# Half of the block sums and differences of a seven-product FFN made on GpSimd instead of VectorE, with every step's place in the issue list laid anew

## The chip, the cores and the metric

One core of a Trainium2 chip runs the whole program. The metric is the time of one execution on the device, in microseconds (us). A measurement of this kernel can tell about 0.5% from no change.

## What is computed

Local attention with a few global keys and a bias that falls with distance, followed by a two-layer FFN with a softplus between the layers. The reference, cut to what matters:

```python
# q, k, v: (4, 8, 768, 64) float32; n_global 8, n_local 96
scores = scale * q @ k.T
keep = (pos_k < n_global) | ((pos_q - pos_k >= 0) & (pos_q - pos_k < n_local))
scores = where(keep, scores + bias, -1e9)
a = softmax(scores)
x = (a @ v) laid out as (3072 tokens, 512)
h = x @ w_in                      # (512, 2048)
g = maximum(h, 0) + log1p(exp(-abs(h)))
out = g @ w_out                   # (2048, 512), float32
```

## The kernel before

The 3072 tokens are 24 blocks of 128 (six to a batch) and 12 chunks of two blocks. A block's attention needs the keys of its own block and the one before it; the eight global keys and values are copied over the first rows of the block before it (steps `gk` and `gv`, lines 271 and 275, small copies on GpSimd, ScalarE or VectorE). For each block and each half of the heads there are scores (`s`, `ss`, TensorE), the bias added (`ab`, `ac`, VectorE), an exponential (`e`, ScalarE), the product with V (`p`, TensorE) and a division by the row sum (`nm`, VectorE, into `xsf`). `xsf` is transposed into `XT` by TensorE or, from block 8 on, by a DMA from SyncE's queue (`y`).

The FFN takes a chunk of 256 tokens. Chunk 0, and the first layer of chunk 1, are made with plain products (`f`, `o`). From there on, both layers cut their matrices into 2 x 2 blocks and make the block product with seven products instead of eight, in the form that shares partial sums. That needs sums and differences of blocks:

- `x_dif` (step `ht`, line 512): four differences of blocks of `XT` to a chunk, 128x256, fp16, for the first layer; each of the four has a single buffer. `x_dif` 2 is made from 1, and 4 from 2.
- `w_sum` (step `hw`): the same of `w_in`, made once.
- `sum` (step `gs`, line 627): four sums and differences of blocks of G to a chunk, 128x1024, fp16, for the second layer; two buffers each. Sum 2 is made from 1, and 4 from 2. Sum 1 goes into output product 5, sum 2 into 6, sum 3 into 7 and sum 4 into 3.
- `w_dif` (step `wd`, line 612): four differences of blocks of `w_out`, in two halves of 128x1024, made once.

The first layer's seven products (step `h`, line 541, eight 128x128 matmuls each, twice per chunk) collect in PSUM; a copy (`hc`) and two additions (`hv`) join them, then exponential (`he`) and logarithm (`hl`) on ScalarE give G. The second layer's products (step `m`, line 657, eight matmuls of 256 columns) are copied (`ec`, ScalarE or VectorE) and added (`ev`, VectorE) into `osb`, which is stored (`st`).

Nothing is scheduled by a compiler. `ORDER` (line 707) is a list of step names, written out; each step appends its instructions to the queues of its engines, and every engine works its queue in that order, waiting by semaphore for what an instruction needs. So the list sets the order on all engines, and with it what stands behind a waiting instruction. A step's last number often chooses the engine. `BANKS` (line 187) tells which of three PSUM banks each temporary takes.

Loads of q, k, v and of the weights (`lq`, `lk`, `lv`, line 102, `wi`, `wo`) are issued from GpSimd's queue. To hold them back, a gate (step `g`, line 705) copies one element of G on GpSimd and so waits until that part of G is there.

Of the kernel before, what the change touches and what calls it, by code (L numbers as in the profile page):

```python
# [20 lines left out]
def kernel(  # L21
# [157 lines left out]
    def bias_part(half, part):  # L179
# [8 lines left out]
        "01201201210212012012012012102101200220201011021010112121010212210101211202210221"  # L188
        "011020201002110121120202112001221002"
# [313 lines left out]
    def x_dif(c, i):  # L503

        HD[c, i] = sums.tile([P, KH, P], F16, tag=f"x_dif{i}", name=f"x_dif{i}", bufs=1)
        a, b = {
            1: lambda: (x_block(c, 0, 1), x_block(c, 0, 0)),
            2: lambda: (x_block(c, 1, 1), HD[c, 1][:]),
            3: lambda: (x_block(c, 1, 1), x_block(c, 0, 1)),
            4: lambda: (x_block(c, 1, 0), HD[c, 2][:]),  # L510
        }[i]()
        nc.vector.tensor_tensor(HD[c, i][:], a, b, ALU.subtract)
# [105 lines left out]
    def g_sum(c, i):  # L618
# [8 lines left out]
        nc.vector.tensor_tensor(SM[c, i][:], a(), b(), op)  # L627
# [74 lines left out]
    def gate(s):  # L702
# [10 lines left out]
        fe1 nm3.0 wo0 nm3.1 s4.0 lv5 x3 wi6 f3 xc3.0 fe3 f9 ab4.0 s4.1 fe9 ab4.1 f0 wo1 t5 kc5.0
        e4.0 f8 qc5.0 gk5.1 s5.0 fe0 f2 ab5.0 f11 fe8 e4.1 gv4.0 wo2 fe2 e5.0 s5.1 fe11 f10 lp0
        p4.0 f13 hw1.0 fe10 hw2.0 f5 fe13 f4 lp1 nm4.0 p4.1 ab5.1 fe4 nm4.1 e5.1 fe5 hw3.0 f12
        gv5.2 x4 p5.0 lp4 nm5.0 o0 p5.1 lq6 nm5.1 xc4.0 lk6 hw1.1 wo3 fe12 o4 x5 f15 xc5.0 lp6
        wd1.0 f14 lp5 f7 ht2.1 fe14 fe15 lk7 h2.1.0 ht2.2 lq7 o1 hw4.0 wd1.1 fe7 hw3.1 hw2.1 lv6
        ht2.4 lq8 hc2.1.0.1 hw4.1 f6 h2.6.0 lp7 gs1.1 wd3.0 gs1.3 h2.2.0 fe6 lp2 o5 gs1.2 ht2.3
# [153 lines left out]
```

## Time and profile before

| | us |
|---|---|
| three runs | 203.16, 201.97, 202.85 |
| median | 202.85 |
| the profiled execution | 203.91 |
| its span, first to last instruction | 201.8 |

The granted clock of TensorE was 0.997 of full speed in that execution. The profile names the engines PE (TensorE matmuls), PEld (its weight loads, which run beside the matmuls), DVE (VectorE), ACT (ScalarE), POOL (GpSimd) and SP (SyncE). A row of a group gives line, engine, operation, output <- input, shape, count, then busy time and mean duration in ns, then the idle time before it. Durations overlap a little: an engine starts its next instruction before the last one's result has landed, so what an instruction costs an engine is the distance to the next start.

### The profile page before, as it was taken

What the parts mean: (1) busy time and instruction counts of PE and PEld (TensorE: products, weight loads), DVE (VectorE), ACT (ScalarE), POOL (GpSimd) and SP (SyncE); (2) the same over time, 40 slices, a digit from 0 to 9 for tenths busy, and PEclk for the clock granted to TensorE, in tenths of its full rate; (3) what the DMA queues carried; (4) which work ended last, traced back from release to release, by engine and by line L of the source; (5) the groups of instructions that cost most, each with busy time, mean ns of one, the idle gap of its engine ahead of it and who ended that gap; (6) DMA issues with size and microseconds to landing.
All of it is one profiled execution on the core that took longest, in us unless ns stands there. A gap on an engine that the chain in (4) does not pass through costs nothing.

```text
span 201.8 us, 6676 instructions
## 1 busy us (share of the span) xinstructions
PE 194.4 (96%) x2729; PEld 167.9 (83%) x2729; DVE 173.8 (86%) x403; ACT 173.5 (86%) x278; POOL 85.3 (42%) x142
## 2 busy tenths in 40 slices
PE   7989999999999999999999999989999999999993
PEld 2657887867989989989998998969999999999992
DVE  7557776999999999989999999979999998867571
ACT  2767699989999999999999999997999998898700
POOL 8997906860574648095264835451003110000000
PEclk9999999999999999999999999999999999999998
DMA  8999999999999999999999999999442512601123
GB/s 126 153 156 169 149 196 207 188 173 158 149 115 157 120 174 195 102 158 158 157 161 180 168 177 167 100 119 145 100 133 44 94 29 30 209 3 54 54 71 138
DMA packets 110622, 26.91 MB, mean 133 GB/s; under 512 B 101760, under 2 KB 108288, under 8 KB 110592
## 3 DMA queue, kind: packets, MB, share of 16 engines
q0 software_dynamic: 78080, 13.37, 98.3%
q1 hardware_dynamic: 31472, 12.85, 36.8%
q8 instruction: 21, 0.34, 0.7%
q10 hardware_dynamic: 1040, 0.26, 0.6%
q14 instruction: 9, 0.07, 0.2%
HBM read 27.26 MB, written 6.29 MB: 166 GB/s over the span
## 4 chain that ended last, share of the span: by engine, by line
PE 59%; DVE 20%; ACT 11%; DMA 5%; issue 3%; DVEq 0%; ACTq 0%
PE o L657 24%; PE hT L541 12%; PE p_ps L541 6%; PE hT L434 5%; PE x_ps L380 3%; DMA XT<-xsf 3%; ACT e_sb L571 3%; DVE sum L627 3%; ACT Pb L364 3%; PE s_ps L284 2%; DVE Z L353 2%; DMA k_f<-in_k_dram 2%; ACT G L575 2%; DVE w_dif L612 2%; DVE xsf L398 2%
## 5 line engine op out<-in xcount | busy, mean ns | idle before, releaser
L575 ACT ACTIVATE G<-e_sb 128x1024 f16<-128x1024 f32 x40 | 41.7, 1061 | 0.1
L541 PEld LDWEIGHTS <-w_sum 128*128 128x128 f16 x640 | 39.0, 98 | 3.2 <-issue 0.9
L364 ACT ACTIVATE Pb<-Z 128x1024 bf16<-128x1024 f32 (+1 forms) x40 | 39.9, 1002 | 0.0
L657 PEld LDWEIGHTS <-sum 128*128 128x128 f16 x352 | 32.7, 98 | 4.3 <-issue 0.6
L657 PE MATMUL o<-w_dif,sum 128*128 128x256 f16 x264 | 33.8, 273 | 0.6 <-DVE b L686 0.5
L541 PEld LDWEIGHTS <-w_in 128*128 128x128 f16 x480 | 29.4, 98 | 0.7 <-DMA XT<-xsf 0.2
L657 PEld LDWEIGHTS <-G 128*128 128x128 f16 x272 | 24.9, 98 | 3.1 <-issue 0.2
L571 ACT ACTIVATE e_sb<-hT 128x512 f32<-128x512 f32 x40 | 24.0, 602 | 2.9 <-PE hT L541 2.6
L541 PE MATMUL hT<-x_dif,w_sum 128*128 128x128 f16 x320 | 24.4, 219 | 0.3 <-DVE hT L551 0.3
L541 PE MATMUL hT<-XT,w_in 128*128 128x128 f16 x320 | 24.4, 219 | 0.0
L344 DVE TENSOR_TENSOR Z<-s_ps,biasA 128x1024 f32<-128x1024 f32 x19 | 23.1, 1216 | 1.1 <-PE s_ps L284 1.1
L275 POOL COPY v_t<-v_t 8x520 bf16<-8x520 bf16 x13 | 8.4, 645 | 33.7 <-PE x_ps L380 32.6
L657 PE MATMUL o<-w_out,G 128*128 128x256 f16 x168 | 21.8, 273 | 0.0
L102 POOL DMA_DIRECT2D v_t<-in_v_dram x24 | 21.5, 896 | 0.6 <-issue 0.5
L102 POOL DMA_DIRECT2D q_t<-in_q_dram x23 | 20.6, 895 | 2.2 <-DMA w_out<-in_moe_w_out_dram 1.4
L102 POOL DMA_DIRECT2D k_t<-in_k_dram x23 | 20.6, 900 | 1.6 <-issue 0.8
L398 DVE TENSOR_TENSOR xsf<-x_ps,rcp 128x256 f16<-128x256 f32 x44 | 18.7, 424 | 1.5
L380 PEld LDWEIGHTS <-Pb 128*128 128x128 bf16 x352 | 15.3, 98 | 2.5 <-issue 0.9
L380 PE MATMUL x_ps<-v_t,Pb 128*128 128x65 bf16 x324 | 17.1, 193 | 0.1
L434 PE MATMUL hT<-XT,w_in 128*128 128x256 f16 x128 | 15.6, 273 | 0.0
L566 DVE TENSOR_TENSOR e_sb<-hp,hT 128x512 f32<-128x512 f32 x20 | 13.6, 682 | 2.3 <-PE hT L541 2.3
L627 DVE TENSOR_TENSOR sum<-G 128x1024 f16<-128x1024 f16 x22 | 15.1, 687 | 0.0
(113 smaller groups left out, 381.4 us busy)
## 6 DMA issues: line engine op xcount, KB each, us to landing
out_dram<-osb SPq DMA_DIRECT2D x18, 256.0 KB, 4.1
v_t<-in_v_dram POOLq DMA_DIRECT2D x24, 128.0 KB, 5.9
k_t<-in_k_dram POOLq DMA_DIRECT2D x23, 128.0 KB, 5.9
q_t<-in_q_dram POOLq DMA_DIRECT2D x23, 128.0 KB, 5.8
w_out<-in_moe_w_out_dram POOLq DMA_DIRECT2D x4, 512.0 KB, 11.2
out_dram<-osb SPq DMA_DIRECT2D x10, 128.0 KB, 2.0
w_in<-in_moe_w_in_dram POOLq DMA_DIRECT2D x4, 256.0 KB, 7.1
w_in<-in_moe_w_in_dram POOLq DMA_DIRECT2D x2, 512.0 KB, 9.1
```

The costliest lines, as they stand in the source:

```text
L102: nc.gpsimd.dma_start(dst[n][:, :, 0:D], src[b, :, i * P : (i + 1) * P, :].rearrange("h s d -> s h d"))
L344: nc.vector.tensor_tensor(Z[:], buf[:, 0:8, :], biasA[:, half, :, :], ALU.add)
L364: nc.scalar.activation(Pb[:, 0:nreg, :], src, AF.Exp, scale=inv_sqrt)
L380: nc.tensor.matmul(x_b[:, lh, :], Pb[:, r, :], v_t[n - t][:, h, :], start=(t == 0), stop=(t == 1 or first),)
L398: nc.vector.tensor_tensor(xsf[:, h0 : h0 + 4, :], x_b[:, :, 0:D], rcp[:, h0 : h0 + 4][:, :, None].to_broadcast([P, 4, D]), ALU.mult,)
L434: nc.tensor.matmul(hT[:, j, :], w[:, m, fo : fo + P], XT[c][:, m, :], start=(j == 0 and m == 0), stop=(m == KM - 1), skip_group_check=(j > 0),
L541: nc.tensor.matmul(o[:, b, :], lhs(k, b), rhs[:, k, :], start=(i in (1, 5) and b == 0 and k == 0), stop=(k == KH - 1), skip_group_check=True,)
L566: nc.vector.tensor_tensor(t, HS[c, "p", u][:], HT[c, "x", u][:], ALU.add)
L571: nc.scalar.activation(o, t, AF.Exp)
L575: nc.scalar.activation(g_tile(c)[:, b0 : b0 + HB, :], HS.pop((c, i, u))[:], AF.Ln, bias=1.0)
L627: nc.vector.tensor_tensor(SM[c, i][:], a(), b(), op)
L657: nc.tensor.matmul(o, lhs[:, k, :], rhs(k)[:, c0:c1], start=(i in (1, 2, 5) and k == 0), stop=(k == NU - 1), skip_group_check=(i not in (1 ...
```

## The change

A new helper chooses between two engines, and `x_dif`, `w_dif_part` and `g_sum` get an argument for it. 18 of the 40 `x_dif`, 2 of the 8 `w_dif` halves and 22 of the 44 sums now have a 1 there. All other work is the same in kind and number; the list and the banks are written anew, and some steps' choice between VectorE, ScalarE and GpSimd changes with it (14 of the 40 `hc` copies are on VectorE instead of 7, and 10 of the small K and V copies instead of 2).

```diff
+    def sum_by(pool):
+        return nc.gpsimd.tensor_tensor if pool else nc.vector.tensor_tensor
...
-    def x_dif(c, i):
+    def x_dif(c, i, by=0):
...
-        nc.vector.tensor_tensor(HD[c, i][:], a, b, ALU.subtract)
+        sum_by(by)(HD[c, i][:], a, b, ALU.subtract)
...
-    def w_dif_part(i, part):
+    def w_dif_part(i, part, by=0):
...
-        nc.vector.tensor_tensor(t[i], a, b, ALU.subtract)
+        sum_by(by)(t[i], a, b, ALU.subtract)
...
-    def g_sum(c, i):
+    def g_sum(c, i, by=0):
...
-        nc.vector.tensor_tensor(SM[c, i][:], a(), b(), op)
+        sum_by(by)(SM[c, i][:], a(), b(), op)
...
-        p19.0 he8.11.0 ht8.4 hl7.1.1 m6.7 hv8.6.0 h8.7.0 nm19.0 hv8.7.0 ss20 ac20.0 p19.1 ab20.0
+        p19.0 h8.2.0 gs6.3.1 ht8.4.1 hc8.5.0.0 he8.11.0 m6.7 hl7.1.1 lq22 hv8.6.0 ec6.7.1 nm19.0
```

In the last line `gs6.3.1` is sum 3 of chunk 6 on GpSimd, and `m6.7` the product that takes it.

GpSimd's queue before, where the loads of block 23 are issued, around the sums of chunk 7 (`KT` and `v_t` copies are the small copies, `gate_t` the gates):

```order
L102 DMA k_t_89<-in_k_dram 128x8x64
L102 DMA q_t_83<-in_q_dram 128x8x64
L271 COPY KT<-KT 128x4x8
L275 COPY v_t_95<-v_t_94 8x520
L705 CAST gate_t<-G 1x1 x3
L275 COPY v_t_90<-v_t_94 8x520
L705 CAST gate_t<-G 1x1
L102 DMA v_t_92<-in_v_dram 128x8x64
```

The same place now; `sum_3209` and `sum_3238` are sums 1 and 2 of chunk 7, `sum_3358` is sum 4 of chunk 6, and the two `x_dif` are differences 3 and 1 of chunk 9:

```order
L102 DMA q_t_82<-in_q_dram 128x8x64
L102 DMA k_t_88<-in_k_dram 128x8x64
L708 CAST gate_t<-G 1x1 x3
L630 TENSOR_TENSOR sum_3209<-G 128x1024
L274 COPY KT<-KT 128x4x8
L278 COPY v_t_95<-v_t_94 8x520
L630 TENSOR_TENSOR sum_3238<-sum_3209,G 128x1024
L515 TENSOR_TENSOR x_dif_3281<-XT 128x256
L515 TENSOR_TENSOR x_dif_3305<-XT 128x256
L630 TENSOR_TENSOR sum_3358<-G,sum_2870 128x1024
```

Three sums and two differences now stand among the loads, gates and small copies, and what follows them on that queue follows their waits.

VectorE's queue before at sums 4 of chunk 6 and 1, 2, 3 of chunk 7 (`sum_3132`, `sum_3154`, `sum_3231`, `sum_3256`):

```order
L627 TENSOR_TENSOR sum_3132<-G,sum_2919 128x1024
L395 RECIPROCAL rcp<-x_ps 128x4
L398 TENSOR_TENSOR xsf<-x_ps,rcp 128x256
L627 TENSOR_TENSOR sum_3154<-G 128x1024
L566 TENSOR_TENSOR p_ps<-hp,hT 128x512
L353 TENSOR_TENSOR Z<-o,biasA 128x512
L627 TENSOR_TENSOR sum_3231<-sum_3154,G 128x1024
L627 TENSOR_TENSOR sum_3256<-G 128x1024
```

The same place now; of those four only sum 3 of chunk 7 (`sum_3234`) is left on VectorE:

```order
L356 TENSOR_TENSOR Z<-s_lo,biasA 128x512
L347 TENSOR_TENSOR Z<-s_ps,biasA 128x1024
L356 TENSOR_TENSOR Z<-o,biasA 128x512
L557 COPY hp<-p_ps 128x512
L569 TENSOR_TENSOR p_ps<-hp,hT 128x512
L630 TENSOR_TENSOR sum_3234<-G 128x1024
L569 TENSOR_TENSOR e_sb<-hp,hT 128x4x128
L356 TENSOR_TENSOR Z<-o,biasA 128x512
```

A copy of a product's block (`hp`) stands there that ScalarE made before, and three sums are gone from it; the one left has two inputs in SBUF, as `sum_3209` and `sum_3238` on GpSimd have, and stands between them in the list.

More of the change, by code (lines that the diff above doesn't have):

```diff
@@ L713 @@
[L713 to L718, printed above, removed]
@@ new lines @@
+        m1.2.1 h2.2.1 d8 nm6.0 p6.1 e7.1 hc2.5.1.1 ev1.2 nm6.1 e7.0 h2.6.1 g7 m1.6 hv2.6.1 p7.0
+        g15 he2.11.1 x6 gs1.4.0 lv8 he2.22.0 nm7.0 d9 hl2.1.0 h2.7.1 ec1.6.1 xc6.0 h2.3.1 p7.1
+        ss8 lq10 hv2.7.1 h2.4.1 m1.7 nm7.1 he2.12.1 ab8.0 he2.22.1 lk11 he2.21.1 lq11 ec1.7.0
+        gk9.2 gv8.2 x7 hl2.0.1 h3.1.0 xc7.0 ac8.1 m1.4 lv9 ac8.0 ss9 d10 ec1.4.0 e8.0 p8.0 ac9.0
+        st0.1 lq15 e8.1 ht3.1.1 ac9.1 nm8.0 h3.5.0 ht3.2.1 hc3.1.0.1 m1.5.0 hc3.5.0.1 h3.6.0
+        hl2.1.1 h3.2.0 d11 he3.11.0 ev1.5 hv3.6.0 m1.3 ab9.0 lq13 h3.3.0 ht3.3.1 h3.1.1 ev1.3
@@ new lines @@
+        gk10.0 p8.1 gv9.0 e9.1 lq12 h3.7.0 he3.12.0 hc3.1.1.1 e9.0 ht3.4.1 nm8.1 m2.1.0 h3.2.1
+        he3.11.1 hv3.7.0 gs2.1.1 h3.4.0 lk12 p9.0 lv10 h3.6.1 gs2.3.0 g21 nm9.0 h3.5.1 he3.21.0
+        gs2.2.0 p9.1 ec2.1.1 ss10 he3.22.0 m2.6 nm9.1 hc3.5.1.1 y8 hv3.6.1 hl3.0.0 st0.0 h3.3.1
+        ab10.0 ec2.6.1 h3.7.1 ac10.1 m2.7 he3.12.1 lv11 e10.0 y9 gv10.2 ec2.7.1 hl3.0.1 ac10.0
+        gk11.2 ss11 gs2.4.1 lk13 lv12 hv3.7.1 ac11.0 ac11.1 h4.1.0 d12 e10.1 m2.4 h3.4.1 p10.0
+        ec2.4.1 he3.22.1 m2.2.1 hc4.1.0.1 ab11.0 nm10.0 he3.21.1 m2.5.0 lq14 ht4.1.0 ev2.2
@@ new lines @@
+        h4.2.0 e11.0 g27 lk15 g23 p10.1 he4.11.0 g13 gv11.0 h4.5.0 d13 ht4.2.1 ev2.5 nm10.1
+        h4.6.0 hc4.5.0.1 ht4.3.1 m2.3 gv18 hv4.6.0 p11.0 lq17 h4.7.0 ev2.3 nm11.0 e11.1 h4.3.0
+        hv4.7.0 ss12 ht4.4.1 p11.1 h4.4.0 hl3.1.1 hl3.1.0 ac12.0 nm11.1 gs3.1.0 he4.12.0 h4.1.1
+        m3.1.0 he4.21.0 ab12.0 hc4.1.1.1 h4.5.1 gs3.2.0 h4.6.1 h4.2.1 he4.22.0 hc4.5.1.1 y10
+        e12.0 gs3.3.1 ec3.1.0 m3.6 ac12.1 lk14 he4.11.1 lv13 lk16 g11 st1.1 y11 e12.1 p12.0
+        st1.0 hv4.6.1 ss13 h4.7.1 nm12.0 h4.3.1 ac13.0 ec3.6.1 gk14.0 hl4.0.0 m3.7 gs3.4.1
@@ new lines @@
+        hv4.7.1 p12.1 h4.4.1 ht5.1.1 g17 hl4.1.0 h5.1.0 lq16 he4.12.1 ac13.1 ec3.7.0 he4.22.1
+        m3.4 st2.0 ht5.3.0 ht5.2.0 he4.21.1 hc5.1.0.1 d14 ab13.0 ht5.4.0 lv14 hl4.1.1 h5.5.0
+        lq18 hc5.5.0.0 m3.5.1 ev3.5 h5.6.0 hl4.0.1 hv5.6.0 nm12.1 e13.0 h5.2.0 gs4.1.0 d15
+        he5.11.0 m3.3 lk17 h5.7.0 h5.3.0 ev3.3 p13.0 y12 ss14 hv5.7.0 nm13.0 e13.1 h5.4.0
+        he5.12.0 h5.1.1 g19 ec3.4.1 ac14.1 he5.22.0 gs4.2.1 m3.2.0 lq19 ac14.0 ab14.0 h5.5.1
+        p13.1 he5.21.0 ev3.2 hc5.1.1.1 e14.1 lk18 hc5.5.1.0 h5.2.1 h5.6.1 he5.11.1 hv5.6.1
@@ new lines @@
+        gv14.0 m4.1.0 e14.0 nm13.1 d16 ec4.1.1 hl5.1.0 gk15.2 ss15 gs4.4.0 h5.7.1 m4.6 hv5.7.1
+        hl5.0.0 ec4.6.1 h5.3.1 st2.1 he5.12.1 ac15.0 gs4.3.1 ac15.1 p14.0 h5.4.1 h6.1.0 nm14.0
+        m4.2.1 ab15.0 y13 gk16.0 ht6.1.0 hc6.1.0.1 e15.1 m4.7 p14.1 lv17 h6.2.0 ht6.2.0 g37
+        ec4.7.0 ht6.3.0 he5.21.1 h6.5.0 he5.22.1 lv15 lq20 h6.6.0 lq21 he6.11.0 m4.4 ev4.2
+        ht6.4.1 hc6.5.0.1 d17 ss16 nm14.1 hl5.0.1 hv6.6.0 y14 gk17.0 h6.7.0 ec4.4.1 g43 ac16.0
+        h6.3.0 lv16 m4.5.0 e15.0 hv6.7.0 hl5.1.1 h6.4.0 gv13 g31 ac16.1 h6.1.1 gv15.0 gs5.3.1
@@ new lines @@
+        ev4.5 m4.3 ab16.0 he6.12.0 ev4.3 lk20 d18 p15.0 he6.21.0 hc6.1.1.1 ss17 e16.0 st3.0
+        nm15.0 gs5.1.0 h6.2.1 e16.1 gs5.2.0 p15.1 nm15.1 m5.1.0 st3.1 y15 he6.11.1 h6.6.1
+        ec5.1.1 h6.5.1 m5.6 ac17.0 gv16.1 p16.0 ac17.1 hc6.5.1.1 st4.0 h7.1.0 gk13 hv6.6.1
+        he6.22.0 ec5.6.1 h6.3.1 h6.7.1 g29 e17.1 lv18 g39 nm16.0 p16.1 ab17.0 he6.12.1 m5.7
+        hv6.7.1 m5.5.1 hc7.1.0.0 lk19 g25 hl6.0.0 lk21 ec5.7.1 gs5.4.1 nm16.1 gv17.2 d19 ev5.5
+        ht7.1.0 h6.4.1 e17.0 h7.2.0 ht7.2.1 he6.22.1 lv19 p17.0 he6.21.1 m5.3 y16 h7.5.0 h7.6.0
@@ new lines @@
+        nm17.0 he7.11.0 ev5.3 hl6.1.0 g33 ss18 m5.4 ht7.3.1 hl6.0.1 hc7.5.0.0 ht7.4.1 d21 g51
+        gk18 hv7.6.0 ac18.1 p17.1 ac18.0 g35 ab18.0 hl6.1.1 e18.1 h7.7.0 h7.3.0 he7.12.0 g47
+        hv7.7.0 gs6.1.1 nm17.1 ss19 g45 h7.4.0 h7.1.1 ac19.0 ec5.4.1 ac19.1 he7.21.0 gs6.2.0
+        m6.1.0 hc7.1.1.1 h7.5.1 h7.2.1 lk23 gk20.2 e18.0 hc7.5.1.0 h7.6.1 lv20 y17 m5.2.1
+        hl7.0.0 p18.0 e19.1 hv7.6.1 ab19.0 h7.7.1 hv7.7.1 lq23 ec6.1.1 h7.3.1 ev5.2 lv21 m6.6
+        nm18.0 h7.4.1 he7.22.0 d20 he7.11.1 ht8.3.1 h8.1.0 ht8.1.0 he7.12.1 p18.1 e19.0 he7.21.1
@@ new lines @@
+        ac21.0 ht9.1.1 he8.22.0 ec7.6.1 he8.21.1 h9.1.0 m6.5.1 hc9.1.0.1 nm20.0 h9.5.0 ab21.0
+        ev6.5 p20.1 hc9.5.0.0 gk22.1 gs6.4.1 h9.2.0 e21.0 e21.1 ht9.2.0 nm20.1 he8.22.1 gv21.2
+        st5.1 he9.11.0 m6.3 ev6.3 g49 h9.6.0 hl8.1.0 m7.7 lv23 hl8.0.1 p21.0 lv22 ht9.4.0 ss22
+        hv9.6.0 ec7.7.0 h9.3.0 d23 nm21.0 m7.4 he9.12.0 h9.7.0 ab22.0 g65 p21.1 ac22.0 hv9.7.0
+        gk23.2 ec7.4.1 m7.2.0 hl8.1.1 h9.4.0 e22.0 gs7.4.1 ac22.1 gs8.1.1 nm21.1 gv22.2 ev7.2
+        ss23 ac23.0 gs8.2.1 he9.21.0 ac23.1 y21 h9.5.1 hc9.5.1.1 y20 h9.1.1 hc9.1.1.1 m7.5.0
@@ new lines @@
+        h9.6.1 ev7.5 g59 m8.1.1 st6.1 hv9.6.1 e22.1 p22.0 hl9.0.0 h9.2.1 ec8.1.1 h9.7.1 st7.1
+        he9.22.0 nm22.0 h9.3.1 m8.6 hl9.1.0 p22.1 he9.12.1 hv9.7.1 h9.4.1 ab23.0 he9.11.1
+        he9.21.1 e23.0 g63 ht10.1.0 ht10.2.0 gv12 nm22.1 ec8.6.1 h10.1.0 gs8.3.1 m7.3 e23.1
+        hc10.1.0.0 gv23.2 h10.5.0 h10.6.0 hc10.5.0.0 m8.7 hv10.6.0 ev7.3 ht10.3.0 he9.22.1 g61
+        ec8.7.1 p23.0 h10.2.0 st6.0 nm23.0 g73 hl9.0.1 h10.3.0 h10.7.0 ht10.4.1 he10.12.0
+        hv10.7.0 p23.1 m8.2.0 he10.11.0 h10.4.0 nm23.1 ev8.2 h10.1.1 hl9.1.1 h10.5.1 m8.5.0
@@ new lines @@
+        gs8.4.0 g69 he10.21.0 gk12 y22 hc10.5.1.1 gs9.1.0 y23 gs9.2.1 hc10.1.1.1 m8.4 hl10.0.0
+        ev8.5 ec8.4.1 h10.6.1 hv10.6.1 ht11.1.0 h10.2.1 m9.1.1 ec9.1.0 g67 he10.11.1 h10.7.1
+        h10.3.1 m8.3 ht11.2.0 h11.1.0 hv10.7.1 gs9.4.1 he10.22.0 he10.12.1 h10.4.1 ev8.3
+        he10.21.1 m9.6 hc11.1.0.0 h11.6.0 ec9.6.1 st8.1 hl10.0.1 h11.5.0 gs9.3.0 he10.22.1
+        h11.2.0 m9.7 ht11.4.0 m10.1.0 hc11.5.0.0 hv11.6.0 ht11.3.0 h11.7.0 ec9.7.0 hl10.1.0
+        hl10.1.1 hv11.7.0 m9.4 gs10.1.0 ec9.4.0 h11.3.0 ec10.1.0 he11.11.0 gs10.2.0 h11.4.0
@@ new lines @@
+        he11.12.0 he11.21.0 h11.1.1 m9.5.1 hc11.1.1.1 h11.5.1 ev9.5 hl11.0.0 hc11.5.1.0
+        he11.22.0 h11.6.1 st8.0 m10.6 hv11.6.1 st7.0 h11.2.1 ec10.6.0 h11.7.1 he11.11.1 gs10.3.0
+        hv11.7.1 h11.3.1 m9.3 ev9.3 h11.4.1 he11.12.1 gs10.4.0 he11.22.1 m10.7 m9.2.1 ec10.7.0
+        m10.4 ev9.2 hl11.1.0 he11.21.1 m10.5.1 hl11.0.1 hl11.1.1 gs11.1.0 ev10.5 ec10.4.1
+        m11.2.2.1 m11.1.0 m10.3 gs11.2.0 ev10.3 gs11.3.1 st9.1 st9.0 ec11.1.1 m11.6 gs11.4.1
+        m10.2.1 ec11.6.1 ev10.2 gk19 m11.7 ec11.7.0 m11.5.1 m11.4 ev11.2.1 ev11.5 st10.0
@@ L794 @@
+        st11.0.1 m11.2.2.0 m11.3 st10.1 ev11.2.0 ec11.4.1 st11.1 ev11.3 st11.0.0
     """
```

103 lines of the change are left out of this document (22 added, 81 removed).

## The prediction

> **What bounds the kernel now.** I read the page's head first, then busy time by stretch.
>
> ```profile
> span 201.8 us, 6676 instructions
> PE 194.4 (96%) x2729; PEld 167.9 (83%) x2729; DVE 173.8 (86%) x403; ACT 173.5 (86%) x278; POOL 85.3 (42%) x142
> ```
> ```profile
> core 0: us, PE busy (x) PEld busy (x) DVE busy (x) ACT busy (x) POOL busy (x), PEclk, DMA share, GB/s
> 50.00:158.00 108.00, 106.40 (x1678) 96.77 (x1673) 103.74 (x227) 104.58 (x170) 50.14 (x90) 1.00 1.67 142
> 158.00:202.00 44.00, 40.44 (x521) 37.61 (x518) 31.42 (x68) 30.21 (x48) 1.37 (x5) 0.99 0.23 73
> ```
>
> From 50 to 158 us (output product 1 of chunk 1 to that of chunk 8) TensorE, VectorE and ScalarE are all busy 96 to 99%, and GpSimd 46%. After 158 VectorE is busy 71% and TensorE has the say, so less VectorE work there is worth little. A busy TensorE is not a full one; the chain of waits gives what a step takes when nothing holds it (start us, us, what):
>
> ```profile
> 65.61 0.87 PE o L657 x8
> 66.48 0.89 PE hT L541 x16
> 68.57 0.24 PE x_ps L380 x8
> ...
> 155.37 0.33 PE s_ps L284 x8
> ...
> 155.93 0.98 PE o L657 x8
> ...
> 158.04 0.87 PE o L657 x8
> ```
>
> The list has, between those two products, in both kernels alike, 100 first-layer products (0.89/2 = 0.445 us each), 48 output products (0.87), 32 P.V steps (0.24, five at a batch's start half), 16 score steps (155.93 - 155.37 = 0.56, two of them half) and two transposes (0.2): 44.5 + 41.8 + 7.1 + 8.4 + 0.4 = 102.2 us. So TensorE loses 5.8 us of 108 there. That is the most that relief of VectorE and ScalarE in this stretch can bring. Where GpSimd waits, by the list of waits (us in total, times, longest):
>
> ```profile
> POOL v_t L275 <- PE x_ps L380: 32.6, 8, 9.0
> POOL KT L271 <- PE o L284: 24.5, 7, 5.3
> POOL gate_t L705 <- ACT G L575: 16.4, 5, 5.0
> ```
>
> Its idle time is 73 us of waiting, in order, for copies and gates whose data is not there yet; it is free time only if something can be put ahead of those waits.
>
> **The change, part by part.** *What VectorE loses and gains.* Groups by shape (busy, mean ns), and a run without waits from the timeline:
>
> ```profile
> L627 DVE TENSOR_TENSOR sum<-G 128x1024 f16<-128x1024 f16 x22 | 15.1, 687 | 0.0
> L512 DVE TENSOR_TENSOR x_dif<-XT,x_dif 128x256 f16<-128x256 f16 x20 | 5.7, 284 | 0.1
> L554 ACT COPY hp<-p_ps 128x512 f32<-128x512 f32 x15 | 8.8, 590 | 0.4 <-PE p_ps L541 0.2
> L554 DVE COPY hp<-p_ps 128x512 f32<-128x512 f32 x5 | 3.4, 684 | 0.3 <-PE p_ps L541 0.3
> ```
> ```profile
> 42.12 0.68 DVE L627 TENSOR_TENSOR sum<-G 128x1024 f16<-128x1024 f16 x1
> 42.72 0.68 DVE L627 TENSOR_TENSOR sum<-sum,G 128x1024 f16<-128x1024 f16 x1
> 43.32 0.28 DVE L512 TENSOR_TENSOR x_dif<-XT 128x256 f16<-128x256 f16 x1
> 43.53 0.68 DVE L566 TENSOR_TENSOR p_ps<-hp,hT 128x512 f32<-128x512 f32 x1
> ```
>
> From start to start a sum costs VectorE 0.60 us and an x_dif 0.21. By the orders, 22 of 44 sums, 18 of 40 x_dif and 2 of 8 w_dif halves go to GpSimd. Between the two products the count on VectorE falls from 25 sums, 28 x_dif and 1 w_dif to 11, 12 and 0: 14 x 0.60 + 16 x 0.21 + 0.60 = 12.4 us. The new list also moves work the other way: 5 more copies of a 128x512 block (0.60 each) leave ScalarE for VectorE, and 7 more of the small K and V copies leave GpSimd and ScalarE for it (about 0.2 each, as the x_dif, the shortest row here): 4.4 us back. Net relief of VectorE 8.0 us of 103.7; ScalarE loses 5 x 0.59 = 2.9 of 104.6.
>
> *What a sum costs on GpSimd.* No row shows a two-input operation there. The nearest are its copies (min/median/max ns):
>
> ```profile
> L275 POOL COPY v_t<-v_t x13: 607/611/1069, 14.1 to 159.6; 8x520 bf16<-8x520 bf16 x13
> ```
> ```profile
> L271 POOL COPY KT<-KT x12: 201/211/437, 14.9 to 138.0; 128x32 bf16<-128x32 bf16 x12
> ```
> ```profile
> L705 POOL CAST gate_t<-G x32: 177/179/499, 50.3 to 165.3; 1x1 bf16<-1x1 f16 x32
> ```
> ```profile
> L102 POOL DMA_DIRECT2D v_t<-in_v_dram x24: 876/885/958, 3.2 to 154.2; - x24
> ...
> DMA to landing us min/median/max: 3.5/5.9/10.6
> ```
>
> (611 - 211)/(520 - 32) = 0.82 ns per element and 0.185 us fixed. One pass over 1024 elements gives 1.02 us, two passes (one per input) 1.86, three (the result too) 2.70; for an x_dif 0.39, 0.60 or 0.81. I take 1.86 and 0.60, since two tensors must be read, and keep the others as ends. The Trainium skill, "GPSIMD Engine Reference", section 3.1, gives 4497 ns for an add of 2048 fp32; half of it, an estimate of 2.25 us, would bring the sum below to about 209 us.
>
> *Fill of GpSimd.* In the stretch it gets 16 sums, 2 w_dif and 16 x_dif: 18 x 1.86 + 16 x 0.60 = 43.1 us, beside 43 loads x 0.89, 27 gates x 0.19, 7 K copies x 0.21 and 6 V copies x 0.61 = 48.6. Together 91.7 us of 108, or 85%; by the high price 61.6 + 48.6 = 110.2, more than the stretch. Each sum waits in the queue for G, for its partner and for a free buffer, and loads, gates and copies stand behind it. A load lands 5.9 us after its issue and is listed well ahead of its use, so I cost late loads at nothing; with the high price that cover is gone.
>
> *The meeting of the two engines.* Two places of the timeline, VectorE and GpSimd:
>
> ```profile
> 104.98 0.67 DVE L627 TENSOR_TENSOR sum<-G,sum 128x1024 f16<-128x1024 f16 x1
> ...
> 112.35 0.82 DVE L627 TENSOR_TENSOR sum<-G 128x1024 f16<-128x1024 f16 x1
> 113.09 0.68 DVE L353 TENSOR_TENSOR Z<-s_lo,biasA 128x512 f32<-128x512 f32 x1
> ```
> ```profile
> 105.06 1.07 POOL L275 COPY v_t<-v_t 8x520 bf16<-8x520 bf16 x1
> ...
> 112.02 0.61 POOL L275 COPY v_t<-v_t 8x520 bf16<-8x520 bf16 x1 [3.82 <-PE x_ps L380]
> ```
>
> The copy that began 0.08 us into a sum took 1.07 instead of 0.61, that is, it stood until the sum was nearly done. The sum that began 0.28 us before the end of a copy took 0.82 instead of 0.68. The maxima of the K copy (437 ns) and the gate (499) point the same way: whichever comes second waits for the first. The Trainium skill, "SBUF — State Buffer", section "Who interferes with whom", makes it a rule: with two inputs in SBUF, VectorE's instruction and a GpSimd one that reads SBUF exclude each other, and the second blocks until the first finishes. The trace agrees for the copy; the sum was held 0.14 us, less than the 0.28 that the whole of the copy would give.
>
> Now the holder would be three times longer. GpSimd's 43.1 us are 40% of the stretch, and 23 two-input operations (11 + 12) stay on VectorE. One that arrives at random during a GpSimd one waits on average (18 x 1.86^2 + 16 x 0.60^2)/(2 x 43.1) = 0.79 us: 23 x 0.40 x 0.79 = 7.3 us. By the low price it is 23 x 0.23 x 0.43 = 2.3 us, by the high one 23 x 0.57 x 1.15 = 15 us. The middle value takes back 7.3 of the 8.0 us of relief, and as waits at places where the list has none.
>
> *Later sums.* A sum that took 0.68 us from start to end takes 1.86. In the list eight of the GpSimd sums stand at most 2.4 us of TensorE work ahead of their product: none ahead of product 7 of chunk 6, one 0.45 us product ahead of product 3 of that chunk, 1.1 to 2.4 us for the others. If each started where it stands, the shortfalls would be 1.86 + 1.41 + 0.74 + 0.3 + 0.1 + 0.1 = 4.5 us. But a place in the list is not yet a start. In the kernel before, sum 2 of chunk 10 stands directly ahead of product 6, and yet nothing waited (VectorE's timeline, then the chain of waits):
>
> ```profile
> 182.07 0.69 DVE L627 TENSOR_TENSOR sum<-sum,G 128x1024 f16<-128x1024 f16 x1
> ```
> ```profile
> 182.21 1.75 PE o L657 x16
> ```
>
> Product 6 is the second half of those 16 matmuls: it began 1.0 us after the sum, since TensorE was one product behind. Counting 0.9 us for that leaves 0.96 + 0.51 = 1.5. I take the middle, 3 us, and it falls on TensorE, the engine that sets the end.
>
> *Other stretches.* Up to 50 us, two w_dif halves, a sum and an x_dif leave VectorE, and loads and first products come in another order; the page gives no sign for it, and I take 0. After 158 us VectorE is idle 29% of the time, so its relief there brings nothing; the two sums of chunk 11 on GpSimd are needed only after other products: 0.
>
> **Sum.** The profiled execution took 203.9 us, its span 201.8 and 2.1 around it; the three timed runs have a median of 202.85. VectorE 0 (8.0 - 7.3, and what is left is not enough to move TensorE), ScalarE 0, late sums +3.0: 206.9 against 203.9, or 205.9 against the median. I put 206.
>
> **Rivals.** *A, the forecast:* the exclusion eats the relief and late sums add 1.5 to 5.5 us: 204 to 208.5. For it speaks the 1.07 us copy; against it, that its meetings are counted as random, and the order may keep them apart.
>
> *B, faster:* the sums cost GpSimd about one pass and rarely meet VectorE's. Then VectorE gains 8.0 - 2.3 = 5.7 us and ScalarE 2.9, and TensorE gets back more than half of its 5.8 us, 3.4: 199.5 (197 to 201.8). It decides once the waits of VectorE's 23 operations stay under some 3 us in total. For it speak VectorE's and ScalarE's 96% and 97% and GpSimd's 46%; against it, the two slowed rows.
>
> *C, no change:* relief and waits cancel, and the sums come early enough: 202 to 203.8.
>
> *D, GpSimd becomes the bound:* at 2.70 us a sum it has 110.2 us of work in a stretch of 108, and not all of its waiting for TensorE (57 us in all now) can vanish. With 5 to 10 us of it left the stretch takes 115 to 120, and the whole 210 to 215. For it speak the 85% at the middle price and the copies' 0.82 ns; against it, that a third pass for the result is likely to run beside the reads.
>
> **Chances.** A 0.45, B 0.30, C 0.13, D 0.12. A measurement here tells about 0.5% from no change, 201.8 to 203.9. All of B lies below: faster 0.30. C and the low edge of A (0.04) are the same: 0.17. The rest, 0.41 + 0.12, is slower: 0.53. A alone goes from 204 to 208.5; for 8 in 10 the range runs from 199, leaving out the lower part of B (0.10), to 212.5, leaving out the upper half of D (0.06).
>
> **What would show it.** Right: a GpSimd sum near 1.9 us; VectorE sums and x_dif with means well over 687 and 284 ns, some over 1.5 us; VectorE busy still about 96% from 50 us to product 1 of chunk 8, with fewer instructions; TensorE waiting for sum on GpSimd, at product 7 of chunk 6 first. B is right if those means stay and VectorE falls under 92%; D, if GpSimd is busy over 95% and its loads land late. The forecast is wrong if the sums take 1 us, or if waits of TensorE for GpSimd do not show.

## The result, and the profile after

The changed kernel takes 209.9 us (median; 208.95 to 210.23), the kernel before 202.9 us beside it: 1.035 times as long, with a 95% interval of 1.030 to 1.039. So it is 7.0 us slower; the forecast was 206.0, +3.1 against the median. The granted clock was 1.00 in the profiled execution (208.95) and 0.992 in the other three; up to 1 us of the 7.0 may be that. The page of the changed kernel, and its busy time by stretch (product 1 of chunk 8 now begins at 161.1):

```profile
span 207.1 us, 6708 instructions
PE 193.6 (93%) x2727; PEld 166.9 (81%) x2729; DVE 172.7 (83%) x374; ACT 171.1 (83%) x272; POOL 145.6 (70%) x177
```
```profile
50.00:161.00 111.00, 106.88 (x1686) 97.38 (x1687) 105.33 (x217) 102.91 (x164) 91.92 (x115) 1.00 1.39 135
161.00:207.00 46.00, 41.38 (x534) 38.19 (x531) 31.25 (x62) 29.66 (x48) 14.40 (x14) 1.00 0.24 79
```

VectorE has 29 instructions fewer and is busy for almost the same time, 172.7 us instead of 173.8: what is left on it has become longer. GpSimd's 91.9 us of work in the middle are near the 91.7 that the prediction had summed, in part by luck: durations overlap a little here too, and with the overlap counted twice the moved operations alone took 47.2 us, where 43.1 were summed. The groups by shape say which operations are longer (mean ns behind the comma):

```profile
L630 DVE TENSOR_TENSOR sum<-sum,G 128x1024 f16<-128x1024 f16 x7 | 7.8, 1112 | 0.0
L515 DVE TENSOR_TENSOR x_dif<-XT 128x256 f16<-128x256 f16 x12 | 6.9, 577 | 0.1
L278 DVE COPY v_t<-v_t 8x520 bf16<-8x520 bf16 x4 | 3.4, 848 | 0.4 <-PE x_ps L383 0.4
L569 DVE TENSOR_TENSOR e_sb<-hp,hT 128x512 f32<-128x512 f32 x20 | 13.6, 680 | 1.6 <-PE hT L544 1.5
...
L630 POOL TENSOR_TENSOR sum<-G 128x1024 f16<-128x1024 f16 x11 | 23.4, 2127 | 19.5 <-ACT G L578 17.5 <-ACT G L456 2.0
L515 POOL TENSOR_TENSOR x_dif<-XT,x_dif 128x256 f16<-128x256 f16 x10 | 7.0, 702 | 5.5 <-DVE x_dif L515 2.9 <-PE x_ps L383 1.7 <-issue 0.6
```

A sum on GpSimd takes 2.13 us. Sums, differences and small copies on VectorE have means well over those of the same operation alone; the additions with an input in PSUM (`e_sb`) have not. Taking each VectorE operation against what its kind takes undisturbed in this trace (the median for sums and differences, the shortest for the few copies), sixteen are held, for 12.4 us: sums 4.3, differences 3.6, V copies 2.3, K copies 1.7, `w_dif` 0.5. What TensorE waited for, and then GpSimd (us in total, times, longest):

```profile
PE s_ps L287 <- DVE Z L345: 3.1, 1, 3.1
PE o L660 <- DVE osb L699: 2.1, 2, 1.3
PE hT L544 <- DVE e_sb L569: 1.0, 2, 0.6
PE hT L544 <- DVE hT L554: 0.6, 2, 0.3
```
```profile
POOL sum L630 <- ACT G L578: 17.5, 4, 16.2
POOL sum L630 <- DVE sum L630: 10.1, 3, 6.2
```

Not one wait of TensorE is for a sum on GpSimd. After the first 10 us its waits come to 7.8 us, in the kernel before to 2.2; the spans of the two traces differ by 5.3. Six of the waits, 6.4 us together, are for VectorE and stand behind an operation that was held; the other new ones are of 0.3 us or less, for ScalarE and for a load. The largest, on VectorE, GpSimd and TensorE:

```profile
45.94 3.69 DVE L630 TENSOR_TENSOR sum<-sum,G 128x1024 f16<-128x1024 f16 x1
...
46.02 0.90 POOL L102 DMA_DIRECT2D k_t<-in_k_dram  x1
46.92 2.15 POOL L615 TENSOR_TENSOR w_dif<-w_out,w_out 128x1024 f16<-128x1024 f16 x1
...
51.59 0.40 PE L287 MATMUL s_ps<-QT,KT 64*128 64x128 bf16 x8 [3.12 <-DVE Z L345]
```

The sum on VectorE ends 0.56 us after GpSimd's `w_dif` half, and the score step's bias addition stands behind it, with two of VectorE's own `w_dif` halves between. The second largest is behind one of the small copies:

```profile
112.38 1.88 DVE L278 COPY v_t<-v_t 8x520 bf16<-8x520 bf16 x1
...
111.99 2.12 POOL L630 TENSOR_TENSOR sum<-G 128x1024 f16<-128x1024 f16 x1
...
114.64 1.03 PE L660 MATMUL o<-w_out,sum 128*128 128x256 f16 x8 [1.33 <-DVE osb L699]
```

Where TensorE stands, by the start of its products in the two traces (us, before and after): product 1 of chunk 1 at 50.1 and 52.6, of chunk 8 at 157.9 and 161.1, product 3 of chunk 11 at 197.4 and 202.7. So 2.5 us were lost before the stretch that the prediction reasoned about, 0.7 in it, and 2.1 after it. (The trace of before is of an execution 1 us over the median, that of the changed kernel of one 1 us under it.)

### The profile page after: what moved, and what is told of

It is laid out like the page before. It is cut to its first block, busy times and chain, and to the rows that moved or that the text cites. A ratio compares the mean times of both kernels' runs of the same rounds, so it can differ in the third digit from the quotient of the medians.

```text
span 207.1 us, 6708 instructions
## 1 busy us (share of the span) xinstructions
PE 193.6 (93%) x2727; PEld 166.9 (81%) x2729; DVE 172.7 (83%) x374; ACT 171.1 (83%) x272; POOL 145.6 (70%) x177
## 4 chain that ended last, share of the span: by engine, by line
PE 63%; DVE 18%; ACT 7%; DMA 6%; issue 4%; POOL 1%; DVEq 0%; ACTq 0%
PE o L660 24%; PE hT L544 17%; PE p_ps L544 6%; PE x_ps L383 4%; DMA w_in<-in_moe_w_in_dram 4%; PE s_ps L287 3%; PE hT L437 3%; DVE sum L630 2%; DMA k_f<-in_k_dram 2%; DVE x_dif L515 2%; ACT Pb L367 2%; DVE e_sb L569 2%; DVE Z L347 2%; DVE w_dif L615 2%; DVE v_t L278 1%
## 5 line engine op out<-in xcount | busy, mean ns | idle before, releaser
L630 POOL TENSOR_TENSOR sum<-G 128x1024 f16<-128x1024 f16 x11 | 23.4, 2127 | 19.5 <-ACT G L578 17.5
L544 PEld LDWEIGHTS <-w_in 128*128 128x128 f16 x480 | 28.7, 98 | 3.2 <-DVE e_sb L569 1.1
L287 PEld LDWEIGHTS <-KT 64*128 64x128 bf16 x352 | 10.0, 94 | 8.6 <-issue 5.9
L630 POOL TENSOR_TENSOR sum<-G,sum 128x1024 f16<-128x1024 f16 x7 | 14.9, 2126 | 1.7 <-DVE sum L630 1.6
```

What stands on the lines that cost most here:

```text
L287: nc.tensor.matmul(dst(4 * sub + 2 * mm + t), KT[n - t][rows, m, :], QT[n][rows, m, :], start=not pre and not (whole and (t or mm)), stop= ...
L544: nc.tensor.matmul(o[:, b, :], lhs(k, b), rhs[:, k, :], start=(i in (1, 5) and b == 0 and k == 0), stop=(k == KH - 1), skip_group_check=True,)
L630: sum_by(by)(SM[c, i][:], a(), b(), op)
```

## The experiments

Three theories. *Exclusion:* VectorE's operations are held while GpSimd has one of its two-input ones, and those waits reach TensorE. *Lateness:* the sums come too late from GpSimd. *List:* the new order itself costs it. Times are medians; each ratio is to the kernel before in the same job.

**The list alone, and the engines alone.** The first has the new list with all 42 operations on VectorE, so 42 steps are altered like these:

```diff
-        ... p19.0 h8.2.0 gs6.3.1 ht8.4.1 ...
+        ... p19.0 h8.2.0 gs6.3.0 ht8.4.0 ...
```

The second has the old list and banks, with the same 42 on GpSimd:

```diff
-        ... p19.0 he8.11.0 ht8.4 ...
+        ... p19.0 he8.11.0 ht8.4.1 ...
```

> The new list and banks, with all sums and differences on VectorE again. Before 202.9 us, changed kernel 209.9. Exclusion theory (VectorE's operations that need the shared path stand still while GpSimd reads): the 12.3 us of stretched VectorE operations in the changed kernel's trace fall to under 1 us, VectorE has 18 us more of its own work, and the time is 203 to 206 us. Lateness theory (a sum takes 2.13 us on GpSimd instead of 0.68, and its product waits): also 203 to 206. List theory (the new list itself is worse, whoever makes the sums): 208 to 211.

> The old list and banks, with the same 42 sums and differences on GpSimd. Exclusion theory: VectorE's remaining two-input operations meet GpSimd's at random; 7 to 12 us of stretched operations, 206 to 212 us. Lateness theory: 206 to 212 as well, but with TensorE waiting for sum or x_dif on GpSimd by name. List theory: no change, 202 to 204.

Measured: 212.5 us, 1.048 (1.041 to 1.054), and 219.7 us, 1.085 (1.078 to 1.092). Both are worse than the change itself and above what any of the theories gave. The new list is written for a VectorE that is rid of those operations; with them VectorE is busy 113.7 of the 120 us from 50 us on. In the old list the 42 operations stand where a GpSimd that works in order can't take them, and there the lateness that I had forecast does show, by name, with V loads that were issued behind sums and differences (second profile, waits):

```profile
PE x_ps L383 <- DMA v_t<-in_v_dram: 4.7, 2, 3.0
PE o L660 <- POOL sum L630: 3.8, 2, 1.9
```

So neither half can be judged by itself: the list's place for the sums is what removed lateness, and what the two cost together needs another cut. Whether the new list by itself costs time is answered further down, by the stand-ins.

**The two w_dif halves back on VectorE.**

```diff
- wd3.1.1 ... wd4.1.1
+ wd3.1.0 ... wd4.1.0
```

> The changed kernel with the two w_dif halves back on VectorE. Exclusion theory: the sum on VectorE that took 3.69 us at 45.9 us takes 0.68, TensorE's wait of 3.1 us for the bias addition at 48 us goes, VectorE pays 1.2 us more: 207 us (206.5 to 208). Lateness theory and list theory: the w_dif halves are needed only by products 7 and 4 of chunk 1, so 209 to 210.5.

Measured: 208.2 us, 1.027 (1.022 to 1.033), just above what exclusion gave and under the other two. The 3.1 us wait is gone; 1.2 us came back as a wait for `xsf` at 53 us, behind the two halves on VectorE. Two operations of 42 gave back 1.7 us by the medians, though no product had waited for them. Up to 1 us of that may be the clock (0.997 to 1.00 here); the spans of the two traces, at 1.00 and 0.998, differ by 1.1.

**The ten small copies.** First back to GpSimd (8) and ScalarE (2), as they were before the change; later all ten on ScalarE, by steps like these:

```diff
-        gk10.0 p8.1 gv9.0 ...
+        gk10.1 p8.1 gv9.1 ...
```

> The changed kernel with the ten small K and V copies that it makes on VectorE given back to the engines that made them in the kernel before (eight to GpSimd, two to ScalarE). Exclusion theory: 3.4 us of stretched copies go (1271 ns at 67.3, 951 at 101.7, 1880 at 112.4), and with them TensorE's waits at 69.1 (0.8 us) and 113.1 (1.5): 207.5 to 208.5 us. Lateness theory and list theory: 209.5 to 210.5, since GpSimd gets 3 us more to do.

> The changed kernel with its ten VectorE copies of K and V on ScalarE. GpSimd's queue stays as it is. Exclusion theory: their 3.9 us of waits are gone and the stops of TensorE behind them at 69 and 113 us (0.78 and 1.50) as well, 207.5 to 208.5. Rivals: what was held at the copy is held at the next two-input operation, 209.5 to 210.5; or ScalarE, at 96% in the middle stretch, becomes later by the ten copies (2 to 3 us), 211 to 213.

Measured: 212.3 us, 1.047 (1.041 to 1.053), and 211.4 us, 1.046 (1.042 to 1.051): both miss, slower than the change. In both a K copy on ScalarE now made TensorE wait 1.1 us near 12 us. In the first the copies were no longer held, but GpSimd's operations moved, and others met (VectorE, then GpSimd):

```profile
71.36 3.65 DVE L630 TENSOR_TENSOR sum<-G 128x1024 f16<-128x1024 f16 x1
...
71.70 0.68 POOL L515 TENSOR_TENSOR x_dif<-XT,x_dif 128x256 f16<-128x256 f16 x1
72.33 2.12 POOL L630 TENSOR_TENSOR sum<-G 128x1024 f16<-128x1024 f16 x1
```

One sum waited for two GpSimd operations in a row, and twice, for 1.4 us in all, TensorE waited for a difference on GpSimd. In the second, a place in the list that suits VectorE did not suit ScalarE, which works in order too: it stood idle ahead of the V copy (the profile names no cause; the copy's data is the likely one), and TensorE behind it (ScalarE, then TensorE):

```profile
69.66 0.62 ACT L278 COPY v_t<-v_t 8x520 bf16<-8x520 bf16 x1 [1.12 <-issue]
...
72.38 0.61 PE L544 MATMUL hT<-XT,w_in 128*128 128x128 f16 x8 [1.44 <-ACT hT L554]
```

But the stretch with the 1.88 us copy did gain: from product 1 of chunk 4 to that of chunk 5 it took 14.6 us, 16.5 in the changed kernel.

**The meetings by themselves.** A small kernel, in one execution, lets VectorE work beside GpSimd sums that follow each other:

```diff
+        ("G", [v_sum] * 8, [g_sum] * 4),
...
+        ("G", [v_dif] * 12, [g_sum] * 4),
+        ("G", [v_copy] * 12, [g_sum] * 4),
...
+        ("G", [p_add] * 12, [g_sum] * 4),
...
+        ("G", [p_add] + [v_sum] * 4, [issue, issue, g_sum]),
```

> A kernel that computes none of the reference: it only lets one engine's instructions meet the other's, in 16 phases. Exclusion theory: a VectorE sum of 128x1024 takes 0.68 us alone and up to 2.13 + 0.68 = 2.8 us when it begins inside a GpSimd sum; an addition or a copy with an input in PSUM (128x512) takes the same 0.68 beside GpSimd sums as alone; the copies 8x520 and 128x32 in SBUF are held like the sums. If the new list and not the engines' meeting stretches them, all take the same alone and in company. Head start: with two load issues ahead of a GpSimd sum, a VectorE sum that begins during the second issue is held until the GpSimd sum ends (over 2.5 us); if an issue does not count, it takes 0.68.

VectorE, first alone and then beside GpSimd (start, us for all, count):

```profile
16.95 2.86 DVE L50 TENSOR_TENSOR v_sum<-a,b 128x1024 f16<-128x1024 f16 x4
19.73 1.26 DVE L56 TENSOR_TENSOR v_dif<-a,b 128x256 f16<-128x256 f16 x4
20.91 1.23 DVE L62 COPY copy_dst<-copy_src 8x520 bf16<-8x520 bf16 x4
22.76 2.12 DVE L71 TENSOR_TENSOR f_out<-f_in,p_in 128x512 f32<-128x512 f32 x3
...
38.20 7.55 DVE L50 TENSOR_TENSOR v_sum<-a,b 128x1024 f16<-128x1024 f16 x3
...
65.08 4.30 DVE L56 TENSOR_TENSOR v_dif<-a,b 128x256 f16<-128x256 f16 x2
...
76.80 6.49 DVE L62 COPY copy_dst<-copy_src 8x520 bf16<-8x520 bf16 x3
...
98.52 2.84 DVE L71 TENSOR_TENSOR f_out<-f_in,p_in 128x512 f32<-128x512 f32 x4
```

A sum takes 2.86/4 = 0.72 us alone and 7.55/3 = 2.5 beside GpSimd; a difference 0.32 and 2.15; a V copy 0.31 and 2.16. The addition with one input in PSUM takes 0.71 in both. In these phases VectorE's sums, differences and V copies each wait for one GpSimd sum, in turns. The Trainium skill, "SBUF — State Buffer", section "Who interferes with whom", has both halves: two inputs in SBUF contend with a GpSimd instruction that reads SBUF, and copies in the modes that use both port pairs do too. The rows agree, though no run here shows the mode in which the small copies ran. The prediction had used the first half only.

One phase asks for the head start seen at 45.94. VectorE's sum, then GpSimd's queue:

```profile
140.73 3.30 DVE L50 TENSOR_TENSOR v_sum<-a,b 128x1024 f16<-128x1024 f16 x1
...
139.58 1.75 POOL L82 DMA_DIRECT2D load<-in_q_dram  x2 [0.27 <-issue]
141.33 2.13 POOL L53 TENSOR_TENSOR g_sum<-c,d 128x1024 f16<-128x1024 f16 x1
```

The sum began 0.6 us before GpSimd's and was still held to its end. With issues alone beside them sums took 0.69. So a GpSimd operation that stands behind an issue holds VectorE from before its own shown start.

**The tail back on VectorE.**

```diff
- gs8.3.1 ... ht10.4.1 ... gs9.2.1 ... gs9.4.1 ... gs11.3.1 ... gs11.4.1
+ gs8.3.0 ... ht10.4.0 ... gs9.2.0 ... gs9.4.0 ... gs11.3.0 ... gs11.4.0
```

> The changed kernel with its last six GpSimd operations that stand in VectorE's way in the tail back on VectorE (sum 3 of chunk 8, difference 4 of chunk 10, sums 2 and 4 of chunk 9, sums 3 and 4 of chunk 11). Exclusion theory: the stretched operations at 165, 176 and 195 us are gone, and with them TensorE's stops of 0.41, 0.54 and 0.91 us: 1.5 to 2.2 us less, 207.7 to 208.4. Lateness or list theory: the tail has spare VectorE time either way and nothing waited for a GpSimd sum there: 209.5 to 210.

Measured: 208.4 us, 1.031 (1.027 to 1.035), at the upper end of what exclusion gave and under the other theories. From product 1 of chunk 8 to product 3 of chunk 11 it took 40.6 us instead of 41.6: less than expected. The stops at 178 and 196 went, but sum 3 of chunk 8, now on VectorE, stands ahead of a copy that TensorE waits for, and that stop grew from 0.41 to 0.88 us.

**GpSimd's sums in four pieces.**

```diff
+        for k in range(0, NU, 2) if by else ():
+            nc.gpsimd.tensor_tensor(SM[c, i][:, k : k + 2, :], a()[:, k : k + 2, :], b()[:, k : k + 2, :], op)
```

> The changed kernel with every GpSimd sum and w_dif half as four instructions of 128x256 instead of one of 128x1024: each holds what they share for some 0.67 us instead of 2.13, and the whole takes 2.5 to 2.7 us. Exclusion theory: a VectorE operation waits for one piece, not for a sum; of the 12 us of waits 4 to 6 are left, and the time is 205 to 207.5. Lateness theory: the sums close 0.5 us later: 211 to 213. If the pieces leave VectorE no gap, nothing changes in the waits: 210 to 212.

Measured: 207.8 us, 1.028 (1.024 to 1.032). The sums are 0.4 us later and the kernel is faster, against lateness (also at the same clock: 207.35 in the profiled execution, 208.95 in that of the changed kernel). But less was gained than expected, since an operation did not always get in at the next border (VectorE, then GpSimd's four pieces):

```profile
133.77 1.97 DVE L515 TENSOR_TENSOR x_dif<-XT 128x256 f16<-128x256 f16 x1
...
133.04 2.54 POOL L634 TENSOR_TENSOR sum<-G 128x256 f16<-128x256 f16 x4
```

That difference waited for three of them. In the small kernel further down, single differences waited for one piece (0.70 to 0.78 us); why it was three here is not settled.

**The meetings that stopped TensorE, thinned.**

```diff
- wd3.1.1 ... wd4.1.1 ... gs9.2.1 ... gs9.4.1 ... gs11.3.1 ... gs11.4.1 ... gv15.0
+ wd3.1.0 ... wd4.1.0 ... gs9.2.0 ... gs9.4.0 ... gs11.3.0 ... gs11.4.0 ... gv15.1
```

> The changed kernel with seven steps altered: w_dif halves 3.1 and 4.1, sums 2 and 4 of chunk 9 and 3 and 4 of chunk 11 back on VectorE, and the V copy at 112 us on ScalarE. These are the meetings that stopped TensorE for 3.3, 1.5, 0.5 and 0.9 us. Exclusion theory: 1.7 (as with the two w_dif halves alone) + 1.2 (tail) + 1.9 (the stretch from product 1 of chunk 4 to that of chunk 5, with the copies on ScalarE) = 4.8 less, 204.5 to 206. Rival, what is taken away at one place is held at another (as with the ten copies): 207.5 to 209. List theory: no gain, 208.5 to 210.

Measured: 204.7 us, 1.010 (1.005 to 1.015), inside what exclusion gave: 5.2 of the 7.0 us are gone with seven steps (the clock was 1.00; against the changed kernel's execution at that clock it is 4.2). Since six of them went back to VectorE, it does not yet separate the holding from where the work lies. One of the stops that are left, 0.7 us at 100 us, is for a DMA into `KT`.

**An operation that does not hold.** A second small kernel, in one execution, with GpSimd fills (memset) in place of sums:

> A kernel that computes none of the reference. GpSimd fills (memset, no input) of 128x1024 and 128x256 by themselves and beside VectorE's sums, differences and the two small copies; then a GpSimd sum in four pieces beside single VectorE operations. Exclusion theory, if it is the reading of two inputs that is shared: a fill holds no VectorE sum (0.69) and no difference (0.29), and the copies perhaps. If any GpSimd work is enough: sums are held as before. Pieces: an operation of VectorE that arrives inside a piece gets in at the next border (at most 0.7 us); or pieces of one sum follow each other too closely, and it waits for two or three.

Beside fills of 0.95 us each, VectorE's sums, differences and V copies:

```profile
22.49 2.86 DVE L50 TENSOR_TENSOR v_sum<-a,b 128x1024 f16<-128x1024 f16 x4
...
28.67 1.91 DVE L56 TENSOR_TENSOR v_dif<-a,b 128x256 f16<-128x256 f16 x6
...
34.73 2.99 DVE L62 COPY copy_dst<-copy_src 8x520 bf16<-8x520 bf16 x3
```

Sums (0.72) and differences (0.32) run as alone, copies (1.0) are held. The same section of the skill says that an operation that only writes does not contend with two inputs; these rows agree.

**Stand-ins of the same length.** Each of the 42 GpSimd operations becomes one element's arithmetic, for the waits, and fills for the time:

```diff
-        sum_by(by)(SM[c, i][:], a(), b(), op)
+        t, a, b = SM[c, i], a(), b()
+        if by:
+            nc.gpsimd.tensor_tensor(t[0:1, :, 0:1], a[0:1, :, 0:1], b[0:1, :, 0:1], op)
+            nc.gpsimd.memset(t[:], 0.0)
+            nc.gpsimd.memset(t[:, 0:7, :], 0.0)
...
```

> The changed kernel with each GpSimd sum, difference and w_dif half replaced by a stand-in in the same place of the list: a subtraction or addition of one element of each block, which keeps the waits for the inputs, and fills (memset) of about the same time in all (0.30 + 1.01 + 0.84 us for a sum, 0.30 + 0.31 for a difference). It leaves the arithmetic of those 42 operations out. A fill holds none of VectorE's two-input operations (0.69 and 0.29 beside it), but it holds the small copies. Exclusion theory: TensorE's stops at 48, 137, 166, 178 and 195 us (3.28, 0.74, 0.41, 0.54, 0.91) vanish and those behind copies (0.78, 1.50) stay: 5.9 less, 203.5 to 205. Lateness or list theory: GpSimd is as long and as late as before and the list the same: 209 to 210.

Measured: 202.1 us, 0.998 (0.995 to 1.001), lower than expected and level with the kernel before. The same groups as above, and VectorE and TensorE where the largest wait had been:

```profile
L646 DVE TENSOR_TENSOR sum<-sum,G 128x1024 f16<-128x1024 f16 x7 | 4.8, 684 | 0.0
L520 DVE TENSOR_TENSOR x_dif<-XT 128x256 f16<-128x256 f16 x12 | 3.4, 285 | 0.5 <-DMA XT<-xsf 0.5
L278 DVE COPY v_t<-v_t 8x520 bf16<-8x520 bf16 x4 | 2.6, 643 | 0.4 <-PE x_ps L383 0.4
```
```profile
45.74 0.68 DVE L646 TENSOR_TENSOR sum<-sum,G 128x1024 f16<-128x1024 f16 x1
...
48.68 0.40 PE L287 MATMUL s_ps<-QT,KT 64*128 64x128 bf16 x8
```

The list is the same, GpSimd is busy 140.5 us instead of 145.6, and the holding of two-input operations is all but gone: 7.8 us less by the medians, of which up to 1 may be the clock (1.00 here). So it is not the new list by itself that costs the time, and not the place of the GpSimd work in it. The copies were held for shorter (a fill is 0.95, not 2.13), which is the likely reason that more went than expected.

**The thinned version, once more.** It puts `wd4.1` on GpSimd again and moves the K copy that was held at 65.7 us, and the V copy behind it:

```diff
- gk10.0 p8.1 gv9.0 e9.1 ... hv3.7.0 gs2.1.1
+ p8.1 e9.1 ... hv3.7.0 gk10.0 gv9.0 gs2.1.1
```

> The thinned version with two more steps altered: w_dif half 4.1 on GpSimd again (back on VectorE behind 3.1 it made TensorE wait 1.2 us for xsf at 53 us), and the K copy held at 65.7 us put, with the V copy behind it, after the addition that TensorE waited for (0.78 us at 67.5). Exclusion theory: 0.6 to 1.2 for the first and 0.5 to 0.8 for the second, 202.8 to 203.6, level with the kernel before. Rival, held elsewhere: 204.3 to 206.

Measured: 204.4 us, 1.011 (1.006 to 1.016): in the range of the rival, held elsewhere, and no gain over the version that it alters. The 0.78 us stop at 67.5 went and the stop at 53 us fell from 1.38 to 0.78, but product 1 of chunk 8 came only 0.6 us earlier, and 5.1 us of held operations are left (5.6 in the version that it alters), 1.3 of them at one difference at 132 us. What the last 1.5 to 2 us of the thinned versions are was not settled.

## Why the prediction was off

**Right in part.** The exclusion is the cause, and it eats the relief and more. VectorE in the middle stretch is busy 94.9% (forecast about 96) with fewer instructions, the means of its sums and differences as a whole are over 687 and 284, four operations took over 1.5 us, and GpSimd is not the bound. But in the sum the exclusion only cancelled the relief, 8.0 - 7.3, and was put at 0; the whole +3 was late sums. That the sign came out right was luck.

**The step that failed: "late sums +3.0".** Measured 0: TensorE waits for no GpSimd sum, though one takes 2.13 us and not 1.86 (the estimate of 2.25 us was nearer, but its 209 us, near the measured time, is partly lateness too). Each of the 22 ended at least 0.9 us before its product. Where the prediction saw it first, at product 7 of chunk 6 (GpSimd's sum, then TensorE's product):

```profile
135.12 2.11 POOL L630 TENSOR_TENSOR sum<-G 128x1024 f16<-128x1024 f16 x1
```
```profile
139.60 1.04 PE L660 MATMUL o<-w_dif,sum 128*128 128x256 f16 x8
```

No work of TensorE stands between the two in the list, and yet TensorE came to the product 4.5 us after GpSimd had begun the sum. I counted the shortfall from places in the list, and took the middle between that (4.5 us) and what a row of the kernel before spoke for (1.5). The row pointed the right way, since the lists run ahead of TensorE, but the 1.5 that it left was too much as well. TensorE's waits for GpSimd by name showed with the old list (3.8 us for sums, 1.6 for differences) and, for differences alone, with the copies moved (1.4 and 0.3). By the prediction's own test, the forecast was wrong in this.

**"Other stretches: 0" failed as well.** They gave 4.6 of the 5.3 us by which the spans of the two traces differ: 2.5 before product 1 of chunk 1, most of it one stop behind a `w_dif` half, and 2.1 in the tail. That VectorE has spare time after 158 us says that relief is worth nothing there; it does not say that a hold is worth nothing. Two holds there, of 1.0 and 1.6 us, made TensorE wait for 0.75 and 0.38 us.

**The meetings were mis-sized by kind and place.** In the middle I had 7.3 us for 23 two-input operations. There it was 1.9 for those and 3.5 for K and V copies, which I had priced at 0.2 us each and not as things that can be held; 4.0 were ahead of the stretch and 3.0 behind it. The total, 12.4, is well over the 7.3, and TensorE's waits behind held operations come to 6.4 us.

**The relief, 8.0 us, was worth little to TensorE.** Rival B gave it 3.4 us without the holding. With that all but gone the whole is 0.998 of before (0.995 to 1.001), at most 1 us less, though 2.7 us of held copies were left. In the traces the middle stretch took 105.8 us with the stand-ins and 107.8 before, but that execution of before was 1 us over its median. So the sum "8.0 - 7.3" was of two things that TensorE does not feel alike: of the relief it felt at most 1 us, and a wait at one place, as at 46 us, reaches it whole. Why the relief brought so little was not tested.

## What to carry over

Before moving a two-input operation from VectorE to GpSimd, count every VectorE operation with two inputs in SBUF and every small 2-byte copy in SBUF as one that may stand for the whole GpSimd operation, 2.1 us here, and at worst for two (3.65 us in one run), and look at who waits behind each place, also where engines are idle. In contact the pair of sums took 2.5 us where VectorE alone needs 1.4 for two, so the move can pay only where the two are kept apart in time; no run here shows one that paid. Judge a new order and a new engine together, and use a stand-in of the same length to take one cause out.

## What the runs showed of the hardware

- A GpSimd sum behind a DMA issue held VectorE from 0.6 us before its own shown start (sum of 3.30 us in the small kernel, 3.69 in the changed one).
- K and V copies on VectorE, one input and 2 bytes, are held as fully as sums (1.99 and 2.16 us beside GpSimd sums), and by GpSimd fills too (1.0).
- GpSimd is held as well when it comes second: its sums took 2.44 us instead of 2.11 in turns with VectorE's sums, its differences 1.00 instead of 0.67.
- ScalarE copies of 128x1024 took 1.04 to 1.05 us beside GpSimd sums, and these 2.12 to 2.13, against 2.11 alone.
